# Attention transposes and feed-forward inputs share two PSUM banks, where each kind had one of its own

## Chip, cores, metric

The program runs on one core of a Trainium2 chip. Times are device microseconds of one execution of the whole program. The core has TensorE (PE in the profile: matmuls; PEld: its weight loads), VectorE (DVE), ScalarE (ACT), GpSimd (POOL) and SyncE (SP, here only issuing DMAs). Each engine works through its own instruction stream in order. PSUM, where PE writes and from where ACT and DVE read, has eight banks of 2 KB per partition.

## What is computed

Attention with a top-32 mask per row (4 batches, 8 heads, 576 rows, head size 64), and then two feed-forward layers on the 2304 token rows, 512 to 2048 to 512, with a rational function in the first and h*cos(h) in the second:

```
scores = scale * np.matmul(q, k.transpose(0, 1, 3, 2))
kth = np.partition(scores, -top_k, axis=-1)[..., -top_k:-top_k + 1]
scores = np.where(scores >= kth, scores, -1000000000.0)
attn = softmax(scores) ; x = (attn @ v), heads side by side
...
h = x @ w_in
g = (a[0] + a[1]*h + a[2]*h2 + a[3]*h3) / (1 + |b[0]|*|h| + |b[1]|*h2 + 1e-6)
x = g @ w_out
...
h = x @ w_in2
out = (h * np.cos(h)) @ w_out2
```

All in float32. The kernel splits every factor into a high and a low part that PE takes at its faster float32 rate, so each product is three matmuls.

## The kernel before

**Attention** goes over 72 units: 18 row tiles of 128 rows, each with 4 pairs of heads. A unit `i` has five pieces in program order. `qk` puts the scores of both heads into the two banks of `sx`, ACT copies them to `sS`. `topk` on DVE finds the 32 largest by four rounds of MAX and three of MATCH_REPLACE on a working tile `e` (of which there are two, `EB=2`), ACT takes Exp into the same `e`, and DVE masks it (SCALAR_TENSOR_TENSOR, with the row sum). `av` one unit later transposes `e` on PE in three parts, `pp{i}a`, `pp{i}b` (four 128x128 blocks each) and `pp{i}t` (one block), each of which ACT copies out to `pt{i}a`, `pt{i}b`, `pt{i}t`; with these PE multiplies into `sx` again (L383, L388). So `e` is free for unit `i+2` when `pp{i}t` has been read. `norm`, twice per block of 256 tokens, transposes the reciprocal row sums into a tile `bc`, which DVE reads when it scales `xs`.

**The feed-forward layers** work on 9 blocks of 256 tokens (`k`), in 8 groups (`g`) of two hidden tiles each. `in1` and `in2` (through `mm_in`, L440 to L442) are 24 matmuls into a tile `h`, which ACT copies to `w` or `hs`; then follow elementwise steps on ACT, POOL and DVE (tiles `w`, `q`, `r`, `u` in the first layer, `hs`, `rr`, `n` in the second), which end in `gg`. `out1` is 24 matmuls (L497 to L499) into `y` (two banks), `out2` 12 matmuls of 512 columns (L554) into `o` (two banks). The weights' low parts and the last layer's weights are streamed from HBM for each group by SP, through four buffers.

**PSUM** holds `sx` (2 banks), `o` (2), `y` (2), one bank for `h` and one for all of `pp` and `bc`. In the first third the weights are converted too (`conv`: `raw`, `cb`, and `diff`, which shares the banks of `o`).

**The order.** The program hands out the pieces of attention and, at step numbers written down for each group (`timed`), the feed-forward pieces. Within that the framework's scheduler orders each engine's stream before the run, by its own estimate of when operands and free buffers are there; a tile of a pool waits in that estimate until one of the pool's buffers is free. The order is fixed once the program is built.

Of the kernel before, what the change touches and what calls it, by code (L numbers as in the profile page):

```python
# [10 lines left out]
F32 = mybir.dt.float32  # L11
# [5 lines left out]
PSUM = bass.MemoryType.PSUM  # L17
# [6 lines left out]
P = 128  # L24
# [10 lines left out]
BT = 2 * P  # L35
# [52 lines left out]
def body(tc, out, qt, kt, vt, ident_d, w1_d, w1o_d, a_d, b_d, w2_d, w2o_d):  # L88
# [4 lines left out]
    with ExitStack() as ctx:  # L93
        def pool(name, bufs=1, **k):
            return ctx.enter_context(tc.tile_pool(name=name, bufs=bufs, **k))
# [6 lines left out]
        mo = pool("mo", 1)  # L102
        dr = pool("dr", 1, space=DRAM)
        ps_s = pool("ps_s", 1, space=PSUM)
        ps_t = pool("ps_t", 1, space=PSUM)
        ps_h = pool("ps_h", 1, space=PSUM)
        ps_o = pool("ps_o", 1, space=PSUM)
        ps_y = pool("ps_y", 1, space=PSUM)

# [167 lines left out]
        def after(mm, bank):  # L277
            for x in order[bank]:
                tc.add_manual_dep(mm.ins, x, mybir.DependencyInfo(mybir.DependencyClass.NoSync, mybir.DependencyReason.DATA), reason="bank")
# [77 lines left out]
        def av(i):  # L357
            n, pr = units[i]
            kvs = ins.pop(i)
            m = P // len(kvs)  # L360
            e = et.pop(i).rearrange("p a c -> p (a c)")
            kb, t, bank = n // 2, n % 2, i % 2
            if i % 4 == 0:
                xst[kb, pr // 2] = mo.tile([P, 2, BT], F32, tag="xs", bufs=XB, name=f"xs{kb}_{pr}")
            xp = sx[:, bank, HALF:HALF + P]

            def tr4(base, nm):
                pp = ps_t.tile([P, 4, P], F32, tag="pt", name=f"pp{i}{nm}")
                for c in range(4):
                    PE.transpose(pp[:, c, :], e[:, base + c * P:base + (c + 1) * P], ident)  # L370
                pt = att.tile([P, 4, P], F32, tag="pts", bufs=2, name=f"pt{i}{nm}")
                A.activation(pt, pp, AF.Copy)
                return pt

            pj = [tr4(0, "a"), tr4(640, "b")]
            pp = ps_t.tile([P, P], F32, tag="pt", name=f"pp{i}t")
            PE.transpose(pp, e[:, 512:640], ident)
            pt = att.tile([P, P], F32, tag="ptt", bufs=1, name=f"pt{i}t")
            A.activation(pt, pp, AF.Copy)
            last = []  # L380
            for c, (_, v) in enumerate(kvs):
                qs = slice(c * m, (c + 1) * m)
                mm = PE.matmul(xp[:, qs], v[:, 512:640], pt[:, qs], start=True, stop=False, skip_group_check=True)  # L383
                after(mm, bank)
                for kc in range(4):
                    for j in range(2):
                        o = xp[j * D:(j + 1) * D, qs]
                        mm = PE.matmul(o, v[:, kc * P + j * D:kc * P + (j + 1) * D], pj[j][:, kc, qs], start=False, stop=(kc == 3), skip_group_check=True)  # L388
                        after(mm, bank)
                        if kc == 3:  # L390
                            last.append(mm.ins.name)
            order[bank] = last
            A.activation(xst[kb, pr // 2][:, pr % 2, t * P:(t + 1) * P], xp, AF.Copy)

        def norm(kb, hf):
            rs = sml.tile([P, 2, H // 2], F32, tag="rs", bufs=2, name=f"rs{kb}_{hf}")
            V.tensor_scalar_add(rs, sums[kb][:, :, 4 * hf:4 * hf + 4], 1e-9)
            V.reciprocal(rs, rs)
            rx = sml.tile([P, 2, 2, P], F32, tag="rx", bufs=1, name=f"rx{kb}_{hf}")
            A.activation(rx.rearrange("p t c (j d) -> p (t c j) d", j=2), rs.rearrange("p t h -> p (t h)").unsqueeze(2).to_broadcast([P, 8, D]), AF.Copy)  # L400
            bc = ps_t.tile([P, 2, BT], F32, tag="pt", name=f"bc{kb}_{hf}")
            for t in range(2):
                for c in range(2):
                    PE.transpose(bc[:, c, t * P:(t + 1) * P], rx[:, t, c], ident)
            yield
            x = xst.pop((kb, hf))
            V.tensor_mul(x, x, bc)
            yield
            if hf == 0:
                xhl[kb] = [mo.tile([P, NCC, BT], F32R, tag=t, name=f"{t}{kb}") for t in ("xh", "xl")]  # L410
            hi, lo = (t[:, 2 * hf:2 * hf + 2] for t in xhl[kb])
            A.activation(hi, x, AF.Copy)
            V.tensor_sub(lo, x, hi.bitcast(F32))
# [223 lines left out]
        def attention():  # L637
# [5 lines left out]
            for i in range(nu + 1):  # L643
# [10 lines left out]
                for p in range(5):  # L654
                    if p == 0 and prev is not None:
                        next(prev)
                    next(t, None)
                    if p == 0:
                        if prev is not None:
                            next(prev)  # L660
                        next(t, None)
                        if prev is not None:
                            av(i - 1)
                            if i % 4 == 0:
                                nrm.append(norm((i - 1) // 8, (i - 1) // 4 % 2))
                                next(nrm[-1])
                                fresh.append(nrm[-1])
                        if 0 < i < nu:
                            load_v(i)
                    if p == LQ > 0 and i % 2 == 0 and i + 2 < nu:  # L670
                        load_q(i + 2)
                    if p == SQ and i % 2 == 0 and 8 <= i + 2 < nu:
                        split_q(i + 2)
                    if fresh and p == 1:
                        next(fresh.pop())
                    if len(nrm) == 2 and (p == 1 or p == 4):
                        next(nrm[0 if p == 1 else 1], None)
                        if p == 4:
                            nrm = []
                    yield  # L680
# [56 lines left out]
```

## Time and profile before

| | |
|---|---|
| runs of the kernel | 1435.71, 1440.75, 1442.73 us; median 1440.75 us |
| profiled execution | 1434.87 us, of which the span from first to last instruction is 1433.1 us |
| PE busy / DVE busy / ACT busy / POOL busy | 1248.5 / 1247.9 / 1080.7 / 632.7 us |
| mean granted clock of PE | 0.934 |

Busy time of PE counts each matmul from its start to its modelled end. Matmuls overlap in the pipeline, so PE's rate is read from the distance of two starts, not from the length of one row.

### The profile page before, as it was taken

Reading aid. Unit: us, or ns where it says so; the run is one execution under the profiler, and the core shown is the slowest. Engines: PE = TensorE matmul, PEld = TensorE weight load, DVE = VectorE, ACT = ScalarE, POOL = GpSimd, SP = SyncE. Lnnn points to the kernel's source line nnn. Section 1 sums busy time; section 2 is a strip of 40 time slices with the busy share of each in tenths; the row PEclk is TensorE's granted clock in tenths of the full one; section 3 lists DMA queues with packets and bytes.
Section 4 is the critical chain, followed back from the end, with each engine's and each line's share of the span. In section 5 each row is a group of like instructions: output and inputs, shape, how many; then the busy total and the mean of one; then the engine's idle time right before and its main releaser. Section 6 shows DMA issues by size and latency. Waiting matters only on the chain.

```text
span 1433.1 us, 24823 instructions
## 1 busy us (share of the span) xinstructions
PE 1248.5 (87%) x8944; PEld 1106.0 (77%) x8944; DVE 1247.9 (87%) x2477; ACT 1080.7 (75%) x1873; POOL 632.7 (44%) x439
## 2 busy tenths in 40 slices
PE   5676777667996999899989988998999999999997
PEld 2344565556985888799878978897998899988986
DVE  6999878899999999999999999999999999645633
ACT  6787788766875887688878786887887788866743
POOL 3657455544543544455555454553545454420000
PEclk9776798779999999999999999999999999999999
DMA  7986867773555656466675665565565777656686
GB/s 242 313 274 206 264 209 223 267 273 126 176 189 188 214 201 217 151 203 236 224 234 203 209 216 168 189 218 178 195 222 198 264 259 277 219 202 221 222 278 220
DMA packets 141547, 314.96 MB, mean 220 GB/s; under 512 B 12016, under 2 KB 28528, under 8 KB 141424
## 3 DMA queue, kind: packets, MB, share of 16 engines
q1 hardware_dynamic: 122832, 261.99, 54.4%
q10 hardware_dynamic: 18592, 51.39, 10.6%
q8 instruction: 70, 1.15, 0.3%
q14 instruction: 53, 0.43, 0.1%
HBM read 278.20 MB, written 35.13 MB: 219 GB/s over the span
## 4 chain that ended last, share of the span: by engine, by line
DVE 41%; PE 31%; ACT 11%; DMA 9%; issue 5%; POOL 2%; ACTq 0%; SPq 0%; DVEq 0%; POOLq 0%
DVE e L78 18%; DVE hd L78 10%; DVE u L78 6%; PE o L554 6%; PE h L440 4%; PE h L441 4%; PE h L442 4%; DVE cb L78 2%; DMA raw<-w 2%; DMA w2o<-w2o 2%; PE y L499 2%; PE y L497 2%; PE y L498 2%; ACT L78 2%; DVE q L78 2%
## 5 line engine op out<-in xcount | busy, mean ns | idle before, releaser
L78 DVE MAX8 hd<-e 128x8 f32<-128x288 f32 (+1 forms) x576 | 322.2, 594 | 0.0
L554 PE MATMUL o<-w2o,gg 128*128 128x512 f32 x864 | 228.7, 402 | 10.4 <-DMA w2o<-w2o 10.3
L78 DVE MATCH_REPLACE8 e<-hd,e 128x288 f32<-128x288 f32 (+1 forms) x432 | 230.6, 538 | 0.0
L554 PEld LDWEIGHTS o<-w2o,gg 128*128 128x128 f32 x864 | 155.7, 192 | 41.8 <-DMA w2o<-w2o 14.1
L78 DVE TENSOR_TENSOR e<-sS 128x576 f32<-128x576 f32 x144 | 164.4, 1178 | 26.9 <-ACT sS L78 13.6
L440 PE MATMUL h<-xh,w1hi 128*128 128x256 f32 x576 | 172.3, 299 | 13.4 <-ACT hs L78 6.4
L497 PE MATMUL y<-gg,w1o 128*128 128x256 f32 x576 | 168.0, 292 | 16.9 <-ACT gg L78 16.9
L440 PE MATMUL h<-x2h,w2hi 128*128 128x256 f32 x576 | 165.8, 288 | 12.3 <-ACT w L78 8.0
L498 PE MATMUL y<-gg,w1o 128*128 128x256 f32 x576 | 167.9, 292 | 6.6 <-POOL gg L78 6.5
L441 PE MATMUL h<-xl,w1hi 128*128 128x256 f32 x576 | 167.9, 292 | 2.3 <-DVE xl L78 2.3
L499 PE MATMUL y<-gg,w1ol 128*128 128x256 f32 x576 | 166.3, 289 | 3.5 <-DMA w1ol<-w1ol 3.4
L78 POOL TENSOR_TENSOR gg<-u,gg 128x512 fp32r<-128x512 f32 x64 | 94.4, 1474 | 169.4 <-ACT gg L78 145.9
L441 PE MATMUL h<-x2l,w2hi 128*128 128x256 f32 x576 | 165.0, 287 | 3.6 <-DVE x2l L78 3.6
L442 PE MATMUL h<-xh,lo 128*128 128x256 f32 x576 | 166.9, 290 | 0.0
L442 PE MATMUL h<-x2h,lo 128*128 128x256 f32 x576 | 164.7, 286 | 0.0
L78 POOL TENSOR_TENSOR u<-u,w 128x512 f32<-128x512 f32 x64 | 94.2, 1471 | 156.6 <-ACT u L78 156.4
L78 DVE SCALAR_TENSOR_TENSOR e<-sS,hd,e 128x576 f32<-128x576 f32 x144 | 140.8, 987 | 10.0 <-ACT e L78 9.7
L78 ACT ACTIVATE e<-sS,nb 128x576 f32<-128x576 f32 x144 | 109.1, 772 | 40.4 <-DVE hd L78 40.3
L78 POOL TENSOR_TENSOR cb<-cb,raw 128x512 int32<-128x512 int32 x64 | 93.7, 1466 | 97.9 <-DVE cb L78 80.5
L497 PEld LDWEIGHTS y<-gg,w1o 128*128 128x128 f32 x576 | 112.6, 195 | 22.3 <-ACT gg L78 20.2
L440 PEld LDWEIGHTS h<-xh,w1hi 128*128 128x128 f32 x576 | 114.0, 198 | 18.6 <-ACT hs L78 8.5
L78 POOL TENSOR_TENSOR rr<-rr,hs 128x512 f32<-128x512 f32 x56 | 79.3, 1436 | 104.0 <-ACT rr L78 103.9
(1166 smaller groups left out, 3720.1 us busy)
## 6 DMA issues: line engine op xcount, KB each, us to landing
w2o<-w2o SPq DMA_DIRECT2D x144, 512.0 KB, 4.2
lo<-w1lo SPq DMA_DIRECT2D x72, 512.0 KB, 4.1
w1ol<-w1ol SPq DMA_DIRECT2D x72, 512.0 KB, 4.1
lo<-w2lo SPq DMA_DIRECT2D x72, 512.0 KB, 4.4
k<-kdr ACTq DMA_DIRECT2D x44, 576.0 KB, 5.1
raw<-w SPq DMA_DIRECT2D x32, 512.0 KB, 5.2
v<-vt ACTq DMA_DIRECT2D x48, 320.0 KB, 4.4
qr<-qt ACTq DMA_DIRECT2D x36, 256.0 KB, 4.2
```

The lines of the kernel that those rows point to most:

```text
L78: r = f(*a, **k)
L440: PE.matmul(h[:, i, :], wh, xh[:, c, :], start=(c == 0), stop=False)
L441: PE.matmul(h[:, i, :], wh, xl[:, c, :], start=False, stop=False)
L442: PE.matmul(h[:, i, :], lo[:, i, c, :], xh[:, c, :], start=False, stop=(c == NCC - 1))
L497: PE.matmul(y[:, c, :], w1o[:, f, cs], gh[:, i, :], start=(f == 0 and c % 2 == 0), stop=False, skip_group_check=True)
L498: PE.matmul(y[:, c, :], w1o[:, f, cs], gl[:, i, :], start=False, stop=False, skip_group_check=True)
L499: PE.matmul(y[:, c, :], wl[:, i, cs], gh[:, i, :], start=False, stop=(f == NF - 1), skip_group_check=True)
L554: PE.matmul(o[:, t, :], l[:, i, ts], wt[i][:, r], start=(f == 0 and r == 0 and l is gh), stop=(f == NF - 1 and l is gl), skip_group_check= ...
```

## The change

The pool `ps_h` goes. `ps_t` gets two banks, and `pp`, `bc` and `h` all carry one tag, so that each new tile of any of these kinds takes one of the two banks. The count of banks is the same, eight. Every instruction stays, with its operands and sizes; only the banks, the waits on them and with them the scheduler's order are others.

```diff
-        ps_t = pool("ps_t", 1, space=PSUM)
-        ps_h = pool("ps_h", 1, space=PSUM)
+        ps_t = ps_h = pool("ps_t", 2, space=PSUM)
...
-                pp = ps_t.tile([P, 4, P], F32, tag="pt", name=f"pp{i}{nm}")
+                pp = ps_t.tile([P, 4, P], F32, tag="h", name=f"pp{i}{nm}")
...
-            pp = ps_t.tile([P, P], F32, tag="pt", name=f"pp{i}t")
+            pp = ps_t.tile([P, P], F32, tag="h", name=f"pp{i}t")
...
-            bc = ps_t.tile([P, 2, BT], F32, tag="pt", name=f"bc{kb}_{hf}")
+            bc = ps_t.tile([P, 2, BT], F32, tag="h", name=f"bc{kb}_{hf}")
```

The file is one line shorter below the pools, so L370 of before is L369 now, and so on.

The streams of PE, DVE, ACT and POOL come out in another order nearly everywhere. Two places on PE follow. Names there carry a running number at the end: `h_5_2_9363` is `h` of the first layer, block 5, group 2; `h_6_5` after a factor `x2h` is the second layer's.

PE's stream before, at the transposes of unit 50, in the middle of the program (between the rows shown stand matmuls of `h` and `y`: 10 `h` and 13 `y` ahead of `pp50b`, then 11 `y` and 24 `h`):

```order
L370 MATMUL pp50a<-ident,e_9114 128x128 x3
L299 MATMUL sx<-k_3_9111,qh_9242 128x288
L370 MATMUL pp50a<-ident,e_9114 128x128
...
L370 MATMUL pp50b<-ident,e_9114 128x128 x4
L299 MATMUL sx<-k_3_9111,qh_9242 128x288
...
L554 MATMUL o_8490<-w2o_11_9361,gg_5_9247 128x512 x6
L377 MATMUL pp50t<-ident,e_9114 128x128
```

The same place now (left out: 20 matmuls of `y`, four of `sx` and four of `y`):

```order
L369 MATMUL pp50a<-ident,e_9111 128x128 x4
L369 MATMUL pp50b<-ident,e_9111 128x128 x4
L496 MATMUL y_9403<-gg_5_0_9234,w1o 128x256
...
L553 MATMUL o_8487<-w2o_10_9356,gg_5_9244 128x512
L376 MATMUL pp50t<-ident,e_9111 128x128
L553 MATMUL o_8487<-w2o_10_9356,gg_5_9244 128x512 x3
```

Between the first transpose of `pp50a` and that of `pp50t` stood 72 other matmuls, and now stand 29. Over the 72 units the median of this count goes from 54 to 26.

PE's stream before, at the last unit's transposes (unit 71), from which on nothing but feed-forward work is left for PE apart from that unit's own product:

```order
L370 MATMUL pp71b<-ident,e_13461 128x128 x4
L498 MATMUL y_12705<-gg_7_5_13589,w1o 128x256
L499 MATMUL y_12705<-gg_7_5_13589,w1ol_5_13598 128x256
L554 MATMUL o_13447<-w2o_4_13706,gg_2_13595 128x512 x5
L440 MATMUL h_6_5_13785<-x2h_12504,w2hi 128x256
...
L377 MATMUL pp71t<-ident,e_13461 128x128
```

The same place now, with what follows it (left out: the unit's 18 matmuls into `sx`, and the other 23 of `h_7_7`):

```order
L376 MATMUL pp71t<-ident,e_13458 128x128
L553 MATMUL o_13444<-w2o_4_13703,gg_2_13592 128x512 x6
L403 MATMUL bc_1_13692<-ident,rx_1_13690 128x128 x4
...
L439 MATMUL h_7_7_13707<-xh_11988,w1hi 128x256
...
L553 MATMUL o_13444<-w2o_5_13705,gg_2_13592 128x512 x5
L439 MATMUL h_6_5_13782<-x2h_12501,w2hi 128x256
```

Group `h_7_7` (24 matmuls), 19 matmuls of `h_6_5` and 5 of `o` stood ahead of `pp71t` and now stand behind it. At most other units too `pp{i}t` is now ahead of 24 to 72 matmuls of `h` that it followed before.

## Rows read from the trace of the kernel before

**Rows 1.** Stages: length, busy time of each engine (instructions), clock, DMA share, GB/s.

```profile
core 0: us, PE busy (x) PEld busy (x) DVE busy (x) ACT busy (x) POOL busy (x), PEclk, DMA share, GB/s
0.00:300.00 300.00, 208.22 (x995) 146.58 (x995) 257.65 (x521) 228.82 (x431) 160.29 (x118) 0.79 0.76 251
300.00:1240.00 940.00, 862.01 (x6705) 796.92 (x6706) 902.92 (x1821) 737.64 (x1278) 456.11 (x310) 0.97 0.61 208
1240.00:1433.00 193.00, 178.31 (x1247) 162.48 (x1246) 87.36 (x136) 114.24 (x165) 16.28 (x13) 1.00 0.68 228
```

**Rows 2.** The page's chain that ended last, by engine.

```profile
DVE 41%; PE 31%; ACT 11%; DMA 9%; issue 5%; POOL 2%; ACTq 0%; SPq 0%; DVEq 0%; POOLq 0%
```

**Rows 3.** What DVE waited for in 300 to 1240: us in all, times, longest.

```profile
DVE e L78 <- ACT e L78: 8.9, 12, 2.2
DVE e L78 <- ACT sS L78: 7.0, 5, 3.0
DVE u L78 <- POOL u L78: 5.5, 7, 1.4
DVE q L78 <- ACT r L78: 3.8, 2, 1.9
DVE e L78 <- PE pp20t L377: 1.7, 1, 1.7
```

**Rows 4.** Who waited for the line of `pp{i}t` (L377), whole program: us, times.

```profile
DVE e L78: 13.2, 16
```

**Rows 5.** Waits of the whole program, DVE and PE, longest in total first.

```profile
DVE e L78 <- PE pp0t L377: 2.2, 1, 2.2
...
PE h L440 <- ACT w L78: 11.1, 9, 1.8
...
PE h L440 <- ACT hs L78: 7.5, 8, 1.8
```

**Rows 6.** DVE at unit 50, in order of time: start, length, instruction, wait before it.

```profile
904.85 3.53 DVE L78 TENSOR_TENSOR e<-sS 128x576 f32<-128x576 f32 x2 [1.70 <-PE pp50t L377]
```

**Rows 7.** PE at unit 50, the transposes alone, same columns.

```profile
894.19 0.49 PE L370 MATMUL pp50a<-ident,e 128*128 128x128 f32 x3
897.92 0.60 PE L370 MATMUL pp50b<-ident,e 128*128 128x128 f32 x4
904.47 0.27 PE L377 MATMUL pp50t<-ident,e 128*128 128x128 f32 x1
```

**Rows 8.** ACT at unit 50: the copies of `pp50a` and `pp50b`.

```profile
894.96 0.60 ACT L78 ACTIVATE pt50a<-pp50a 128x512 f32<-128x512 f32 x1 [1.34 <-PE pp50a L370]
...
902.93 0.58 ACT L78 ACTIVATE pt50b<-pp50b 128x512 f32<-128x512 f32 x1
```

**Rows 9.** What PE waited for in 1240 to 1433.

```profile
PE o L554 <- DMA w2o<-w2o: 3.0, 5, 0.9
PE y L499 <- DMA w1ol<-w1ol: 2.9, 3, 2.3
PE h L440 <- ACT hs L78: 2.7, 2, 1.7
```

**Rows 10.** PE at `pp71t`, then pieces of the chain in the last 190 us.

```profile
1248.39 0.27 PE L377 MATMUL pp71t<-ident,e 128*128 128x128 f32 x1
...
1246.63 0.12 PE h L440
1246.75 0.12 PE h L441
...
1402.79 2.75 PE o L554 x12
```

**Rows 11.** What PE waited for in 300 to 1240.

```profile
PE h L440 <- ACT w L78: 8.7, 7, 1.8
PE h L440 <- ACT hs L78: 4.8, 6, 1.8
...
PE pp56a L370 <- DVE xs L78: 2.2, 1, 2.2
```

**Rows 12.** What ACT waited for in 300 to 1240.

```profile
ACT hs L78 <- PE h L442: 8.6, 8, 2.3
...
ACT w L78 <- PE h L442: 6.0, 7, 1.8
```

**Rows 13.** What DVE waited for in 0 to 300, the longest.

```profile
DVE cb L78 <- ACT cb L78: 20.9, 11, 3.9
```

## The prediction, made before the changed kernel ran

> **What bounds the kernel now.** I read the stages first [rows 1]. In 300 to 1240 us, where attention and the feed-forward layers run side by side, DVE is busy 902.9 of 940 us (96%) and PE 862.0 (92%); both work through a fixed order, so either can hold up the other. In the last 193 us attention is over, DVE is busy for less than half, and PE for 178.3: there PE and the streams that feed it set the end. In the first 300 us, with the weight conversion, no engine is full: DVE has 42.3 us idle, PE 91.8 and a low clock (0.79). The chain that ended last agrees [rows 2]: DVE 41% of the span, PE 31%. So up to about 1240 us a change is worth what it takes off DVE's waits, and behind that what it takes off or puts onto PE.
>
> Next come DVE's waits in the middle stage [rows 3]. They are small and spread: 8.9 us for Exp, 7.0 for the score copies, 9.3 for feed-forward operands (5.5 and 3.8), and then a list of single waits for `pp{i}t`, the last transposes of a unit, of which the row of 1.7 us is the first. Over the whole program these come to 13.2 us in 16 waits [rows 4], 2.2 of them at unit 0 [rows 5]. They arise because `e` has two buffers: unit 52 can't begin on DVE until unit 50's `e` has been transposed. Unit 50 shows it [rows 6]: DVE stands 1.70 us until `pp50t`. PE started on that unit's transposes at 894.19, and reached `pp50t` only at 904.47 [rows 7].
>
> **The change, part by part.** It adds and removes no instruction, so all of its price lies in waits and in the order.
>
> *Transposes sooner.* With one bank, `pp50b` has to wait for the copy of `pp50a`, and `pp50t` for that of `pp50b`, which ACT ended only at 903.51 (902.93 and 0.58 [rows 8]), 5.6 us after PE began `pp50b`. The scheduler filled these gaps with feed-forward matmuls, 72 between `pp50a` and `pp50t`. Now `pp50b` takes the other bank and `pp50t` only needs the copy of `pp50a`, which was over at 895.56; 29 matmuls are left between them. At 0.12 us from start to start [rows 10] the 43 that go are 5.2 us, against a wait of 1.7 us, which is the longest of its kind outside unit 0. DVE's own order hardly moves: ahead of the last mask of unit 71 stand 186 instead of 187 of the three `u` steps. So I take the 13.2 us less the 2.2 of unit 0, where the data themselves are late: -11.0 us. Bounds: 0, if the next operand (scores, Exp) ends the wait instead; -13.2.
>
> *Banks of h.* PE stands 18.6 us (11.1 and 7.5 [rows 5]) because `h` is still being copied by ACT. In the middle stage it is 13.5 of this [rows 11], in the end stage 2.7 [rows 9]. With two banks the next `h` starts in the other one. Behind PE's wait in the end stage stands everything to the end, so I count the 2.7 in full. In the middle DVE is the fuller engine, and its waits for PE are already counted: 0 there. Bounds 0 and -18.6. `bc` held the transposes' bank until DVE had scaled `xs`; PE waited four times for that, 2.2 us at most [rows 11] and 6.5 in all, off DVE's path for the same reason. Bounds 0 and -6.5.
>
> *Later feed-forward work.* What moves ahead of the transposes is paid back behind them. At `pp71t` 43 matmuls of `h` and 5 of `o` are left over that were done before. A matmul of `h` is 0.12 us and 12 of `o` are 2.75 us, 0.23 each [rows 10]: 43 x 0.12 + 5 x 0.23 = +6.3 us in a stage where PE is the bound. Their streams' order on SP doesn't change. PE waits there 5.9 us for DMA (3.0 and 2.9 [rows 9]), which I leave as it is. Bounds 0, if PE gets to `pp71t` as much sooner, and +6.3.
>
> *New waits.* The three transposes and `h` now compete for two banks: `pp{i}t` stands close behind `pp{i}a`, and an `h` close behind `pp{i}b`. I counted, in both orders, how much PE work at these rates lies between the end of one tile in a bank and the next tile that needs it (now taking the banks in turn): 66 places with less than 2 us before, 43 now. So the new waits should not exceed the old; 0. An eviction takes 0.6 us on ACT but comes as late as ACT's queue makes it, as the 5.6 us above show.
>
> *The first 300 us.* The order of conversions, transposes and the first feed-forward groups is reshuffled most here: before `pp20t` 144 fewer matmuls of `h` now, caught up to 48 six units later. DVE's idle time here is half waits for ACT's part of the conversion, 20.9 us [rows 13], which the banks don't touch. I can't price a reshuffle; half of that row, 10 us, bounds it on either side, and I take 0.
>
> Sum: -11.0 - 2.7 + 6.3 = -7.4 us. On the profiled execution's 1434.87 us (a span of 1433.1 and 1.8 around it) that is 1427.5. That execution lies 5.9 us under the median of the runs, 1440.75, and a new median should be held against the median: 1433.4, say 1433 us, 0.5% faster. I put what a measurement of this kernel can tell from no change at 0.5%, 7.2 us; the forecast stands just there.
>
> **The rivals.**
>
> *PE is the bound in the middle as well.* Then the 13.5 us of `h` waits and the 6.5 of `bc` count too: -7.4 - 20.0 = -27.4, 1413 us. For it: PE stands on 31% of the chain and is 92% busy. Against it: DVE at 96% has only 37 us to give in that stage, and most of its waits name ACT or POOL.
>
> *The feed-forward chain comes too late (slower).* `h` is computed 24 to 72 matmuls, 3 to 9 us, later against attention, and ACT, which works in order, then stands for it with the transposes' copies and Exp behind it. ACT now waits 14.6 us for `h` in the middle (8.6 and 6.0 [rows 12]), and DVE 9.3 us for feed-forward operands. If DVE's 11.0 us return as such waits and the 9.3 double: +9.3 - 2.7 + 6.3 = +12.9, 1454 us. It decides from about 15 us of new waits on DVE on, enough to lift the sum of -7.4 to half a per cent above the old time. Against it: DVE's order puts the same steps a little later too (1 to 6 `u` steps fewer ahead of the units that I compared).
>
> *No change.* DVE's 11 us go over to the next operand in line, the score copies or Exp of [rows 3], and the end stage costs 6.3 - 2.7: +3.6, 1444 us. One of the skill's rules stands with it: the Trainium skill, "TensorE: Matmul & The Clock Gate", section "HAM oscillation — how this bites in real kernels", tells of a kernel for which a second set of PSUM banks, once its loads were in order, gave no further gain (126.6 to 125.5 us). No run here shows it yet; that PE stands only 18.6 us of 1433 for `h` is in its favour.
>
> **How the numbers follow.** Forecast 0.44, with a range of its own from 1424 to 1441 (10 us lower by the first 300 us, 8 higher if DVE's gain is mostly lost): half of it beyond 0.5%. PE bound too: 0.18. Late feed-forward chain: 0.21. No change: 0.17. Faster by over 0.5%: 0.23 + 0.18 = 0.41. Within: 0.21 + 0.15 = 0.36. Slower: 0.21 + 0.02 = 0.23. The range leaves out the lower half of the PE case (below 1414) and the upper half of the late chain (above 1453), some 0.2.
>
> **What would show it.** Right: DVE's waits for `pp{i}t` fall from 13.2 to about 2 us; PE's waits for `w` and `hs` ahead of `h` fall under 5; `pp71t` comes near 1237 us instead of 1248.4, with about 4 us more behind it (6.3 less 2.7) than the 184.7 now. PE as the bound: `pp71t` 20 us or more earlier. Late chain: DVE's waits for `u`, `q`, `rr` in the middle above 20 us, ACT's for `h` above 25. What would make me wrong: a first stage that ends more than 10 us apart from before, or transposes that stand for their own copies, PE waiting for `pt{i}a` ahead of `pp{i}t` in most units.

## The result, and the profile after

The change makes the kernel 1.1% faster: 1424.0 us (median of four runs, 1421.21 to 1426.03) against 1441.74 us before (four runs, 1435.71 to 1443.76), a ratio of 0.9893 with a 95% interval of 0.9867 to 0.9920. The profiled execution took 1421.21 us with a span of 1419.4, against 1434.87 and 1433.1 before: 13.7 us less (17.7 between the medians). The forecast was 7.4 less.

Busy time of the page, after:

```profile
PE 1242.8 (88%) x8944; PEld 1103.0 (78%) x8944; DVE 1218.0 (86%) x2477; ACT 1074.0 (76%) x1873; POOL 610.8 (43%) x439
```

The counts of instructions are the same as before, but DVE is busy for 29.9 us less (1247.9 before) and POOL for 21.9 less (632.7). The prediction has no term for the shorter instructions of DVE. The stages after, in the columns of [rows 1], the last one cut at the shorter span:

```profile
0.00:300.00 300.00, 205.69 (x994) 143.77 (x996) 260.41 (x537) 231.26 (x436) 158.97 (x118) 0.79 0.79 257
300.00:1240.00 940.00, 866.23 (x6770) 801.34 (x6766) 868.70 (x1805) 731.17 (x1278) 436.18 (x310) 0.97 0.62 208
1240.00:1419.00 179.00, 170.93 (x1187) 157.88 (x1186) 88.90 (x136) 111.56 (x160) 15.67 (x12) 1.00 0.72 238
```

In the middle stage DVE runs 1805 instructions instead of 1821, so the 868.70 us can't be held against 902.92 as they stand. A cut at an event that both have is better: the last transpose, `pp71t`, at 1248.39 us before [rows 10] and 1235.81 now. Windows of before up to that point and from it on:

```profile
0.00:1248.40 1248.40, 1078.64 (x7776) 951.61 (x7777) 1163.03 (x2343) 972.65 (x1719) 620.67 (x430) 0.92 0.65 219
1248.40:1433.10 184.70, 169.91 (x1171) 154.37 (x1169) 84.90 (x134) 108.06 (x155) 12.01 (x10) 1.00 0.68 228
```

The same of after:

```profile
0.00:1235.80 1235.80, 1068.43 (x7727) 942.37 (x7728) 1127.99 (x2340) 961.00 (x1710) 592.85 (x426) 0.93 0.66 220
1235.80:1419.40 183.60, 174.42 (x1219) 160.62 (x1217) 90.01 (x138) 113.00 (x163) 17.98 (x13) 1.00 0.71 235
```

Ahead of `pp71t` the time falls by 12.6 us, behind it by 1.1. Ahead of it DVE is busy for 35.0 us less, of which 5.1 moved behind it with a few instructions (84.90 to 90.01 there), and idle for 22.4 us more (85.4 before, the 1248.40 less 1163.03; 107.8 now). So DVE waits more than before and is still earlier, because its instructions take less time. The lead grows over the run and is then partly lost: `pp15t` comes 11.5 us sooner (306.6 to 295.1), `pp29t` 16.2 (551.25 to 535.03), `pp47t` 19.8, `pp61t` 23.9 (1088.40 to 1064.46); in the last ten units 11.4 of it go again, where DVE is busy for 4.4 us less but idle for 15.7 more.

What DVE waited for in 300 to 1240 after, which answers to [rows 3]:

```profile
DVE e L78 <- ACT sS L78: 33.0, 15, 7.6
DVE u L78 <- POOL u L78: 14.1, 8, 8.1
DVE q L78 <- ACT r L78: 10.8, 9, 1.9
DVE e L78 <- ACT e L78: 5.5, 12, 1.0
DVE rr L78 <- ACT n L78: 1.8, 2, 1.3
```

Who waited for the line of `pp{i}t`, now L376, in the whole program, as [rows 4]:

```profile
  DVE e L78: 2.3, 4
```

The wait that the prediction spoke of fell from 13.2 us to 2.3. In its place stands the next operand of the same instruction, the score copy `sS`: 33.0 us in the middle, against 7.0 [rows 3], and 44.3 in the whole program, against 13.6 (some 6.5 of either at the very start). What PE waited for in 300 to 1240, the first row:

```profile
PE o L553 <- DMA w2o<-w2o: 23.9, 15, 3.5
```

and from `pp71t` to the end, all of it:

```profile
PE o L553 <- DMA w2o<-w2o: 3.1, 5, 1.3
```

PE no longer waits for `w` or `hs` ahead of `h` (18.6 us before [rows 5]), only 6.3 us in 11 short waits for `pt{i}b`, whose bank `h` now takes; but it waits for `w2o`, the streamed weights of the last layer, much longer than before (26.3 us in the whole program, 10.3 before). PE also stands longer ahead of `pp{i}a` and `pp{i}b` until DVE has masked `e`: 62.7 us, summed over the trace, against 21.1, two thirds of them in the first 300 us. One of the waits for `w2o` can be followed through three engines. PE:

```profile
930.60 2.90 PE L553 MATMUL o<-w2o,gg 128*128 128x512 f32 x6 [2.83 <-DMA w2o<-w2o]
933.30 0.37 PE L298 MATMUL sx<-k,qh 128*128 128x288 f32 x1
```

ACT:

```profile
933.97 0.63 ACT L78 ACTIVATE qh<-qr 128x512 fp32r<-128x512 f32 x1 [4.54 <-PE sx L298]
934.50 0.63 ACT L78 ACTIVATE sS<-sx 128x576 f32<-128x576 f32 x1
```

DVE:

```profile
935.17 1.42 DVE L78 TENSOR_TENSOR e<-sS 128x576 f32<-128x576 f32 x1 [3.56 <-ACT sS L78]
```

PE stands 2.83 us for the weights with the scores' matmuls queued behind; ACT, which needs these matmuls done, stands 4.54 us with the copy to `sS` behind it; DVE stands 3.56 us for that copy.

And these are the DVE instructions that got shorter, after: mean ns is the second number behind the bar.

```profile
L78 DVE TENSOR_TENSOR e<-sS 128x576 f32<-128x576 f32 x144 | 147.9, 1061 | 46.7 <-ACT sS L78 44.3 <-PE pp40t L376 1.0 <-PE pp68t L376 0.9
L78 DVE SCALAR_TENSOR_TENSOR e<-sS,hd,e 128x576 f32<-128x576 f32 x144 | 137.0, 961 | 7.9 <-ACT e L78 7.7
L78 DVE SCALAR_TENSOR_TENSOR u<-u,nega,w 128x512 f32<-128x512 f32 x72 | 77.4, 1075 | 16.0 <-POOL u L78 16.0
```

The same groups before:

```profile
L78 DVE TENSOR_TENSOR e<-sS 128x576 f32<-128x576 f32 x144 | 164.4, 1178 | 26.9 <-ACT sS L78 13.6 <-PE pp0t L377 2.2 <-PE pp20t L377 1.7
L78 DVE SCALAR_TENSOR_TENSOR e<-sS,hd,e 128x576 f32<-128x576 f32 x144 | 140.8, 987 | 10.0 <-ACT e L78 9.7
L78 DVE SCALAR_TENSOR_TENSOR u<-u,nega,w 128x512 f32<-128x512 f32 x72 | 83.7, 1162 | 8.3 <-POOL u L78 8.1
```

These three give 26.6 of the 29.9 us. All of them have two inputs along their whole length. In the first group it is the number of meetings with GpSimd that fell: before, 91 of the 144 had GpSimd beside them for over 40% of their time and took 1.43 us on average, and 45 met none and took 0.75; now these are 68 at 1.41 us and 70 at 0.75. MAX8 and MATCH_REPLACE8, which have one, take what they took (322.5 us for MAX8 now, 322.9 before).

### The profile page after: what moved, and what is told of

Same layout as the page of the kernel before. It is cut to its first block, busy times and chain, and to the rows that moved or that the text cites. A ratio compares the mean times of both kernels' runs of the same rounds, so it can differ in the third digit from the quotient of the medians.

```text
span 1419.4 us, 24807 instructions
## 1 busy us (share of the span) xinstructions
PE 1242.8 (88%) x8944; PEld 1103.0 (78%) x8944; DVE 1218.0 (86%) x2477; ACT 1074.0 (76%) x1873; POOL 610.8 (43%) x439
## 5 line engine op out<-in xcount | busy, mean ns | idle before, releaser
L553 PE MATMUL o<-w2o,gg 128*128 128x512 f32 x864 | 231.4, 406 | 26.5 <-DMA w2o<-w2o 26.3
L78 DVE TENSOR_TENSOR e<-sS 128x576 f32<-128x576 f32 x144 | 147.9, 1061 | 46.7 <-ACT sS L78 44.3
L496 PE MATMUL y<-gg,w1o 128*128 128x256 f32 x576 | 171.6, 298 | 7.8 <-ACT gg L78 5.3
L497 PE MATMUL y<-gg,w1o 128*128 128x256 f32 x576 | 170.0, 295 | 7.9 <-POOL gg L78 7.9
L498 PE MATMUL y<-gg,w1ol 128*128 128x256 f32 x576 | 169.9, 295 | 2.7 <-DMA w1ol<-w1ol 2.6
L78 POOL TENSOR_TENSOR gg<-u,gg 128x512 fp32r<-128x512 f32 x64 | 97.6, 1525 | 141.8 <-ACT gg L78 73.2
L78 DVE SCALAR_TENSOR_TENSOR e<-sS,hd,e 128x576 f32<-128x576 f32 x144 | 137.0, 961 | 7.9 <-ACT e L78 7.7
L78 POOL TENSOR_TENSOR u<-u,w 128x512 f32<-128x512 f32 x64 | 86.7, 1355 | 100.2 <-ACT u L78 83.4
```

The source lines that it names most:

```text
L78: r = f(*a, **k)
L496: PE.matmul(y[:, c, :], w1o[:, f, cs], gh[:, i, :], start=(f == 0 and c % 2 == 0), stop=False, skip_group_check=True)
L497: PE.matmul(y[:, c, :], w1o[:, f, cs], gl[:, i, :], start=False, stop=False, skip_group_check=True)
L498: PE.matmul(y[:, c, :], wl[:, i, cs], gh[:, i, :], start=False, stop=(f == NF - 1), skip_group_check=True)
L553: PE.matmul(o[:, t, :], l[:, i, ts], wt[i][:, r], start=(f == 0 and r == 0 and l is gh), stop=(f == NF - 1 and l is gl), skip_group_check= ...
```

## The experiments

Three theories were set against each other. *Banks*: the second bank takes waits away, and that is the gain. *Collisions*: DVE's instructions with two input tensors run slower beside GpSimd's, and the new order puts them side by side less. *Chain*: the new order is held back by the `w2o` stream, by way of PE, ACT and the score copies. Where a kernel is called pinned, each engine's instructions are held in a given order, whatever the scheduler would do:

```diff
+        pin(tc, start)    # one dependency from each instruction to the next of its engine, no semaphore
```

**The order alone.** Pools and tags of before, order of after on all engines, except for four matmuls near the end of two tiles of `h`.

```diff
+        pin(tc, start)    # on the program of before, with the order of after
```

> This kernel has the pools of before (one bank for h, one for pp and bc) and the order of the changed kernel, instruction by instruction on every engine (four matmuls in the last 60 us excepted, which would need two h tiles open at once). Order theory: the gain lies in the order that the scheduler wrote, and the second bank does little at run time: 1421 to 1428 us, ratio 0.985 to 0.992, two-input DVE rows as short as after (TENSOR_TENSOR e 1.06 us). Bank theory: in this order pp b stands right behind pp a and pp t behind both, so with one bank PE stands for a copy (1.3 us and more) up to twice in each of 72 units, and the gain needs the second bank: 1440 us or more, ratio 0.999 or above.

Measured: 1510.65 us, 1.0492 of before [1.0462, 1.0522]. Its page, and rows of PE's and DVE's waits in the whole program (this file's helper is L124, `mm_in` L500):

```profile
PE 1260.3 (84%) x8944; PEld 1113.2 (74%) x8944; DVE 1227.5 (81%) x2477; ACT 1083.2 (72%) x1873; POOL 610.9 (40%) x439
```

```profile
PE h L500 <- ACT w L124: 28.2, 24, 3.1
PE h L500 <- ACT hs L124: 10.0, 6, 5.6
```

```profile
DVE e L124 <- ACT sS L124: 50.6, 23, 7.8
```

With one bank for the transposes, `pp{i}b` and `pp{i}t` stand for the copies of the transposes ahead of them: 102.7 us in 80 waits, summed over the trace, where after has 3.4 us in 2. So without the second bank the new order loses 4.9% instead of gaining 1.1. But DVE's busy time, 1227.5 us, lies nearer to after's 1218.0 than to before's 1247.9, though the banks are those of before: most of the shortening seems to come with the order. How much isn't shown, since in a run that is 5% longer DVE meets GpSimd less often anyway; 5% of what DVE loses beside GpSimd in before (155 us, see below) is an estimate of 8 of these 20 us. The third group above, `u`, isn't shorter here (1174 ns, before 1162).

**Two banks in the end stage alone.** Before, with every second `h` of the last block of tokens in the transposes' bank. The order is that of before up to the last eighth of PE's stream.

```diff
-            h = ps_h.tile([P, 2, BT], F32, tag="h", name=f"h{m}_{k}_{g}")
+            own = k < NB - 1 or g % 2 == 0
+            h = (ps_h if own else ps_t).tile([P, 2, BT], F32, tag="h" if own else "pt", name=f"h{m}_{k}_{g}")
```

> Before, with one edit: in the last block (k = 8) the odd groups' h of both layers goes to the bank of pp, which attention no longer needs there. The order of all engines is that of before up to the last 15 per cent of PE's stream (DVE: 6 per cent). Prediction's term for the end stage: PE's 2.7 us of waiting for hs go, 0.998, 1438 us, PE from pp71t to the end 182 us instead of 184.7. Rival: the end is set by the streams from HBM and by PE's own rate, 184.7 us stay, ratio 1.000. A larger share: the end stage shortens by 7 us, as it did after when the 6.3 us of added work are taken off: 0.995.

Measured: 1432.73 us, 0.9958 [0.9937, 0.9980]. `pp71t` is at 1251.8, and 179.0 us follow it, 5.7 fewer than before. PE's waits from there on:

```profile
PE o L555 <- DMA w2o<-w2o: 2.5, 3, 2.0
PE h L443 <- DMA lo<-w2lo: 1.1, 1, 1.1
PE h L443 <- DMA lo<-w1lo: 0.6, 1, 0.6
```

The waits of `h` for its bank are gone, and 5.7 us with them, twice the 2.7 that were counted from [rows 9]. Not all of it need be the bank: the order of the end stage is another too, and PE waits there 4.2 us for streams instead of 5.9.

**Fewer collisions, before and after.** GpSimd's two products of the first layer, q*r and u*w, run on 64 of the 512 columns in the blocks in which GpSimd does them; the other columns are left out. Both kernels are pinned to their own order, so nothing but the length of these 128 instructions changes.

```diff
+            n = DM if E1 is V else 64
-            E1.tensor_mul(q, q, r)
+            E1.tensor_mul(q[:, :n], q[:, :n], r[:, :n])
...
-            E1.tensor_mul(u, u, w)
+            E1.tensor_mul(u[:, :n], u[:, :n], w[:, :n])
```

On before:

> Before, with its own order held fixed on every engine; GpSimd's two products of the first layer (q*r and u*w) work on 64 of 512 columns in blocks 0 to 7, so this leaves out part of the elementwise work and the output is not the reference's. It changes nothing on DVE, PE or ACT themselves, but takes some 170 of GpSimd's 633 us. Contention theory: DVE's two-input rows are longer only while GpSimd runs (TENSOR_TENSOR e 0.72 us without it, 1.38 with it): their mean falls from 1.18 to about 1.05, DVE's busy sum by 25 to 45 us, and the time by 10 to 35 us, 1405 to 1430. Rival: the lengths come from something else, such as a wait inside the row for ACT or PE: DVE's busy sum stays within 8 us of 1248 and the time within 8 us of 1440.

On after:

> The changed kernel with its own order held fixed, and the same cut of GpSimd's two products to 64 of 512 columns as in the third run (part of the elementwise work is left out). If the change gained because its order lets DVE collide less with GpSimd, the cut takes that advantage away: it ends where the cut kernel of before did, 1405 to 1413 us. If the gain lies in banks and waits, the two add up: 0.980 x 0.989 = 0.969, 1396 us or less. Half and half: about 1402.

Measured: on before 1410.06 us, 0.9801 [0.9765, 0.9836]; on after 1411.58 us, 0.9810 [0.9793, 0.9826]. The page of the first:

```profile
PE 1247.6 (89%) x8944; PEld 1106.2 (79%) x8944; DVE 1192.0 (85%) x2477; ACT 1078.2 (77%) x1873; POOL 492.7 (35%) x439
```

POOL has 140.0 us less to do, and DVE, of whose instructions none was touched, is busy for 55.9 us less than in before (25 to 45 were expected). On after it is 1188.0, so the two kernels, 29.9 us apart in DVE's busy time with the products in full, are 4.0 apart without them, and their times can't be told apart. That is what the collision theory says and the bank theory doesn't. One thing is mixed in: shorter products also have `q` and `u` ready earlier, which can shorten other waits, so it isn't shown that the 2% of the first run are all collisions. The waits for the scores remain on after:

```profile
DVE e L124 <- ACT sS L124: 46.8, 19, 6.8
```

Up to `pp71t` the two cut kernels read as follows, in the columns of [rows 1], before first:

```profile
0.00:1216.48 1216.48, 1075.24 (x7776) 949.22 (x7776) 1107.44 (x2344) 970.49 (x1719) 481.12 (x430) 0.93 0.68 224
0.00:1224.83 1224.83, 1064.61 (x7728) 941.51 (x7728) 1098.92 (x2340) 959.64 (x1710) 467.32 (x426) 0.92 0.66 222
```

In these two executions the new order is 8.3 us later at `pp71t`: DVE is busy for 8.5 us less, where it was 35.0, and still idle for 16.9 us more (109.0 and 125.9). So with most of the difference in collisions gone, what is left up to there is the new order's longer waits.

**Half of the `w2o` stream, after and before.** Only the high half of `w2o` is loaded, and stands for the low half too, whose values are left out; instructions and order stay (pinned), and a load moves 256 KB instead of 512.

```diff
-                w2t[k, f] = stream(f"w2o{k}_{f}", w2o[f])
+                t = mo.tile([P, 2, 512], F32R, tag="st", bufs=NST, name=f"w2o{k}_{f}")
+                SP.dma_start(out=t[:, 0].bitcast(F32), in_=w2o[f][:, 0])
+                w2t[k, f] = t
...
-                    PE.matmul(o[:, t, :], l[:, i, ts], wt[i][:, r], ...
+                    PE.matmul(o[:, t, :], l[:, i, ts], wt[i][:, 0], ...
```

On after:

> The changed kernel with its own order held fixed; of each tile of the last layer's weights only the high half is loaded (256 KB for 512), and the matmuls take it for the low half too, so the low part of these weights is left out. Chain theory: in the new order PE stands for w2o ahead of the scores (26.3 us against 10.3 before), ACT behind PE, and DVE for the score copies (44.3 us against 13.6): with the loads halved these fall to about 5 and 20 us, and the time by 12 to 25 us, 1399 to 1412. Rival: the score copies come late by ACT's own queue or by the place of the scores in PE's order; the time stays within 8 us of 1424.

On before:

> The same halving of w2o (the low part of these weights left out), on the kernel before with its own order held fixed. Chain theory: it has little of that wait, so it gains less, 0 to 10 us, 1430 to 1440. Rival, that less traffic helps both kernels alike: as many us as the run of the changed kernel gains.

Measured: on after 1397.71 us, 0.9720 [0.9695, 0.9745]; on before 1428.82 us, 0.9949 [0.9924, 0.9975]. After on half the stream, PE and DVE in the whole program:

```profile
PE o L615 <- DMA w2o<-w2o: 4.5, 6, 1.1
```

```profile
DVE e L124 <- ACT sS L124: 31.1, 16, 6.9
```

By the ratios, the same cut is worth 1.7% on after (0.9893 to 0.9720) and 0.5% on before; the difference is 1.2% or 17 us, give or take 6 by the intervals. That much the `w2o` stream costs after and didn't cost before; that it does so through PE, ACT and `sS` is followed in the trace above, and no run changed that path by itself. Only part of the score waits goes with the stream, and less than was expected: 31.1 of 44.3 us remain (about 20 were to), so other things make PE late for the scores too. Up to `pp71t`, before first, as above:

```profile
0.00:1253.63 1253.63, 1089.32 (x7775) 956.99 (x7776) 1167.12 (x2343) 973.12 (x1719) 621.78 (x430) 0.92 0.59 196
0.00:1217.28 1217.28, 1061.39 (x7727) 935.94 (x7728) 1129.20 (x2340) 959.94 (x1710) 595.22 (x426) 0.93 0.60 202
```

Here the new order reaches `pp71t` 36.3 us sooner, DVE is busy for 37.9 us less and idle for about the same (86.5 and 88.1). So the 22.4 us that DVE is idle for longer in after go with the stream, and the gain that is left is in DVE's busy time. These are single executions; that of before lies 4.5 us above the median of its runs.

**The order shifted by a step.** `S0` is the step of the first feed-forward group; one more puts all feed-forward pieces one step (a fifth of a unit) later against attention, and the scheduler makes another order from it.

```diff
-S0, MD, O1P, I2, O2, SB = 46, 4, 1, 2, 3, 4
+S0, MD, O1P, I2, O2, SB = 47, 4, 1, 2, 3, 4
```

Before with 47, after with 47, before with 45, after with 45, after with 48, before with 48:

> Before, with all feed-forward pieces handed out one step later (S0 47 for 46): no bank changes, but the scheduler reorders all engines. Chance-order theory: a reshuffle of this kind moves the time by about 1 per cent either way: anything from 1425 to 1455, more than 0.5 per cent from before. Theory that the two banks give the 1.1 per cent: 1440 within 0.4 per cent (the one step is a third of a unit, under 4 us of delay).

> The changed kernel with all feed-forward pieces handed out one step later (S0 47). The same step without the shared banks gave 1.0081 of before. If two banks are worth about 1 per cent whatever the order: 1430 to 1439, ratio 0.994 to 1.000. If the gain was the luck of one order: anything, also above 1445.

> Before, with all feed-forward pieces handed out one step earlier (S0 45). A second sample of what a reshuffle alone does: 1425 to 1455; its use is as the partner of the next run.

> The changed kernel with S0 45. If two banks are worth about 1 per cent whatever the order, it is 8 to 22 us below the run of before with S0 45. If the sign depends on the order, the two lie within 7 us or the other way round.

> The changed kernel with the feed-forward pieces two steps later (S0 48). S0 45, 46, 47 gave 1432, 1424, 1396. If a later start leaves the streams of w2o more room, it stays below 1410; if each order is its own case, anything from 1395 to 1435.

> Before with S0 48, the partner of the last run (1444.6 with the shared banks). Theory that two banks shorten DVE's two-input rows by some 35 to 45 us in any order, and that only the new waits decide how much is left: 1449 to 1475, with DVE's busy sum about 1255 to 1265 against some 1220 in its partner. Theory that the sign itself depends on the order: 1445 or less.

Measured, ratios to runs of the kernel before made beside each:

| S0 | banks apart: us, ratio | DVE busy | banks shared: us, ratio | DVE busy |
|---|---|---|---|---|
| 45 | 1439.39, 0.9992 [0.9975, 1.0010] | 1259.2 | 1432.00, 0.9958 [0.9940, 0.9976] | 1224.5 |
| 46 | 1441.74, 1 | 1247.9 | 1424.00, 0.9893 [0.9867, 0.9920] | 1218.0 |
| 47 | 1450.32, 1.0081 [1.0060, 1.0103] | 1257.9 | 1395.96, 0.9702 [0.9674, 0.9729] | 1222.8 |
| 48 | 1446.88, 1.0046 [1.0022, 1.0070] | 1241.0 | 1444.61, 1.0059 [1.0035, 1.0084] | 1231.3 |

Shared banks make DVE less busy in all four pairs, by 9.7 to 35.1 us. What becomes of it depends on the waits of that order: 0.3% at 45, 1.1% at 46, 3.8% at 47 (0.9702 / 1.0081), nothing at 48. So only the sign holds, in that no pair is slower beyond its intervals; the size is the order's. Several results lay outside what was expected: 1396.0 at 47 where two banks worth 1% gave 1430 to 1439, 1444.6 at 48 where 1435 was the most, and before with 48 between its two theories, with 1241.0 us of DVE's busy time where 1255 to 1265 was expected. The best, after with 47, has half of after's waits for the scores and for `w2o`:

```profile
DVE e L78 <- ACT sS L78: 21.0, 17, 7.4
```

```profile
PE o L553 <- DMA w2o<-w2o: 11.8, 17, 1.6
```

With 48 DVE's first wait is another, that for Exp (7.7 us in after), and the first row of PE's waits is for another stream, `w1ol` (2.6 us in after):

```profile
DVE e L78 <- ACT e L78: 35.9, 22, 4.0
DVE u L78 <- POOL u L78: 24.4, 18, 7.1
```

```profile
PE y L498 <- DMA w1ol<-w1ol: 31.7, 30, 2.4
```

No run halved that stream, so what it costs at 48 isn't shown.

After with S0 = 47 beats both kernels: 1396.0 us, 3.0% under before and 1.9% under after.

## Why the prediction was right, and where its sum was not

The direction and the range held; the sum of -7.4 us was too small (-13.7 between the profiled executions), and it was not made up of the right parts: up to `pp71t` the runs show a gain of 35.0 us in DVE's busy time, for which it had no term, and 22.4 us more of DVE's idle time, where it had counted on less. That the difference of the two fell into the range is in part luck. Step by step:

- *"It adds and removes no instruction, so all of its price lies in waits and in the order."* This is the step that failed. The durations of instructions were taken as fixed, but DVE's fell by 29.9 us. The cuts of GpSimd's products show that the length of GpSimd's work sets DVE's busy time, and that with it cut the two kernels are equally fast; the order pinned on the old banks points to the order, more than the banks, as what carries DVE's shorter time. The traces agree in all four pairs: counted against rows of the same kind that meet no GpSimd instruction, DVE's two-input instructions lose 154.9 us in before and 122.0 in after, 32.9 less; at 45, 47 and 48 it is 35.2, 35.4 and 10.5 less, next to 34.7, 35.1 and 9.7 of DVE's busy time. That this is the whole of the gain isn't shown, since the cut also makes operands earlier.
- *Transposes sooner, -11.0.* The mechanism was right: DVE's waits for `pp{i}t` fell to 2.3 us. As time it was worth nothing that can be seen: DVE is idle for 22.4 us more up to `pp71t`, and even with the `w2o` stream halved in both kernels for 1.6 more. This is the bound named there (0, "if the next operand (scores, Exp) ends the wait instead"), and it went beyond it.
- *New waits, 0.* Wrong. I counted places where two tiles compete for a bank, and these are few, as said (3.4 us of transposes and 6.3 of `h` for the copies of transposes, in place of 18.6). The new waits don't come from the banks, but from the `w2o` stream, for which PE now stands longer: 26.3 us instead of 10.3. Through the chain at 930 us above they reach DVE, and cost about 17 us by the two halved streams. I had read PE's waits for DMA at the end only, and left them "as it is".
- *Banks of h, -2.7 in the end stage, and later feed-forward work, +6.3.* Together +3.6 was forecast; the stretch behind `pp71t` got 1.1 us shorter. More work does stand there: PE runs 1219 instructions instead of 1171, the 48 that were counted, and is busy for 4.5 us more, so the 6.3 was too much. What went of PE's idle time there is 5.6 us (4.5 + 1.1), and the run with two banks in the end stage alone gives 5.7. The 2.7 was mis-sized: it took the two waits for `hs` alone. What the rest is made of isn't shown.
- *The first 300 us, 0 within 10.* By `pp15t`, at 295 us, the lead is 11.5 us, just over the bound, and more than 10 us was named as a sign of being wrong. DVE is busy for 8.8 us less up to there: it is the same missing term.
- *The rivals.* PE as the bound in the middle would have `pp71t` 20 us earlier; it is 12.6. The late feed-forward chain was half there: ACT waits 35.2 us for `h` in the middle (26.7 for `w`, 8.5 for `hs`), over the 25 that were to show it, and DVE 26.7 us for `u`, `q` and `rr`, over the 20. So both of its signs came, and it did not decide, because DVE had become faster by more. The result that the Trainium skill, "TensorE: Matmul & The Clock Gate", section "HAM oscillation — how this bites in real kernels", tells of one kernel, that a second set of PSUM banks gave no further gain, has no parallel in the pairs at 45, 46 and 47 here, and one in that at 48.

Left open: why the orders with shared banks cost DVE less, and why that at 48 loses it all to waits. Over the whole traces 315 DVE instructions with two inputs meet a GpSimd instruction before and 274 after; at 48, where DVE's busy time gains least, 299 and 247. There a meeting costs more, 0.57 us on average instead of 0.51, where in the first pair it costs 0.45 instead of 0.49. So the number of meetings doesn't explain the size alone, and no run changed it alone.

## What to carry to other kernels

Where a change moves instructions of DVE against GpSimd's, don't take DVE's durations as fixed: look at how the same instruction's rows differ with and without GpSimd beside it, and price the collisions. A wait that is taken away ends where the next operand ends, so follow the second latest operand through the engines before counting the wait as time. And measure such a change at two or three neighbouring orders: here one step of the schedule (after at 47 instead of 46) was worth more, 1.9%, than the change itself.

## What the runs showed of the hardware

How much an instruction of DVE with two inputs loses beside GpSimd was not expected. Two score instructions of before with no GpSimd instruction near them:

```profile
1220.74 1.42 DVE L78 TENSOR_TENSOR e<-sS 128x576 f32<-128x576 f32 x2
```

They take 0.71 us each from start to end of the pair. The two of [rows 6], at 904.85, take 3.53 us, 1.77 each, and these ran on GpSimd meanwhile:

```profile
904.72 1.27 POOL L78 TENSOR_TENSOR gg<-u,gg 128x512 fp32r<-128x512 f32 x1
905.94 1.82 POOL L78 TENSOR_TENSOR gg<-rr,gg 128x512 fp32r<-128x512 f32 x1
```

GpSimd's own instruction is longer too: the second takes 1.82 us, where the 13 of its 56 kind that meet no such DVE instruction take 1.30 on average. Over the whole trace of before, these DVE instructions, row by row, take 0.75 us on average where they meet no GpSimd instruction (45 of 144) and 1.43 where one is busy for over 40% of their time (91), 1.97 at most; MAX8 takes the same with both (0.74 us on 576 columns). So does `xs<-xs,bc`, whose second input lies in PSUM: 0.67 us with and without. One input alone is no safeguard: TENSOR_SCALAR `cb<-cb` takes 0.41 us where it meets no GpSimd instruction (35 of 64) and 0.98 where one is busy for over 40% of its time (24). The Trainium skill, "SBUF — State Buffer", section "SBUF: two separate sides", says that a DVE instruction with two inputs from SBUF and a GpSimd instruction that reads SBUF share a pair of ports, which one of them holds for its whole length while the other waits. The trace agrees for the two-input instructions, `xs<-xs,bc` included, and in the size: the longest score instruction, 1.97 us, is 1.22 over the 0.75, just under one GpSimd instruction of 1.30.
